# A fused attention and MLP block: three transposes taken from TensorE to VectorE and DMA

## The chip, the cores and the metric

The kernel runs on one core of one Trainium2 chip. The metric is the device time of one execution in microseconds (us). The time before is the median of three runs; the profile is of one further execution.

## The reference

x is one sequence of S = 2048 tokens with D = 576 features, in f32. With `x = layernorm(A_x)` as the common input, the result is a sum of a sliding attention branch and of a mixing and MLP branch:

```python
def _A_ref(x, wqkv, wo):          # 32 heads of 18, window 8, dilation 2
    q, k, v = split(x @ wqkv)     # 576 x 1728
    # each token attends to itself and 7 tokens before it, 2 apart
    attn = softmax(einsum(q, k_gathered) * 18 ** -0.5 + mask)
    return einsum(attn, v_gathered) @ wo

def _B_ref(x, w1, w2, w3, w4):
    h = gelu(layernorm(x) @ w1)               # 576 x 576
    # four quarters of the features, shifted by +1, -1, +2, -2 tokens
    x1 = x + shifted(h) @ w2                  # 576 x 576
    return x1 + gelu(layernorm(x1) @ w3) @ w4 # 576 x 4608, 4608 x 576

xn = layernorm(A_x)
return A_x + _A_ref(xn, wqkv, wo) + _B_ref(xn, w1, w2, w3, w4)
```

## The kernel before, in words

Tokens come in 16 tiles of 128 and in 4 blocks of 512. Every f32 matmul is done as three matmuls of fp32r parts: an operand is split into `hi` (cast on ScalarE) and `lo` (the rest, subtracted on VectorE), and the products hi x hi, hi x lo and lo x hi are added in PSUM. 576 features are four chunks of 128 and a tail of 64; a transposed block `xt` has nine slots: 0 to 3 the `hi` of the chunks, 5 to 8 their `lo`, and slot 4 the tail, `hi` in the upper 64 partitions and `lo` in the lower 64. `PAIRS` (line 35) lists the 14 products, so a group is 14 matmuls, or 28 where two PSUM banks are filled.

Four arrays have to be transposed so that features lie on the partitions: x (normalised), z (normalised again, the input of w1), x1n (x1 normalised, the input of w3) and o (the attention's result, the input of wo). In the kernel before all four go through `transposes` (line 97): four TensorE transposes of 128 x 128 per token tile (line 102), and for every second tile one more for the tails of a pair (line 105), into PSUM; from there a cast on ScalarE (107, 110) and a subtract on VectorE (111, 114) write the nine slots.

The order is written out by hand, one program order for all engines:

- **Q stage** (lines 298 to 347). x is loaded, normalised (`norm_x`), transposed (`prep_x`) and multiplied by wqkv; the result is spilled to DRAM (`spill`, line 217). The first z tiles are normalised and transposed within the last four token tiles (336 to 347). Transposed blocks lie in a ring of two buffers (`ring_block`, 167).
- **Mixing** (422 to 440). Per block, four groups of 14 matmuls (`mix_tile`) and one of 9 for the remainder (`mix_rem`), with two gelus and a subtract each. `mix_rem` returns five small VectorE and ScalarE steps, which `todo` hands out one by one and which fill T4. The z tiles of the next block are transposed in between (429). Mixing uses the two one-bank PSUM buffers `psa`.
- **w2 loop** (481 to 505). Per token tile 28 matmuls, an add onto `Y`, the statistics (`stats`, line 84), and for tiles 6 to 13 the normalising and transposing of x1n (`n_norm`, `n_prep`). The rest of `todo` is handed out here.
- **MLP** (697 to 742). 72 units (18 pairs of hidden chunks x 4 blocks) of two `up` groups (line 612) and the unit before's four `down` groups (625). x1n's tiles 8 to 15 are normalised and transposed in units 0 to 2 (`LATE`, 645). Beside it VectorE computes the attention: a generator (516) hands out its instructions, each with a cost in us; `bg` (597) is called six times per unit with the credit `RATE / 6` and stops when the credit is spent. The generator is opened in unit 1, gets credit from unit 3, and is flushed at unit NU - 4 = 68. Its result goes to DRAM as `od` (554).
- **End** (743 to 768). o's tiles are loaded from `od` (`load_o`), transposed (`prep_o`), x is added to `Y` (695), and per tile 28 matmuls with wo, an add and a store follow.

All DMAs are issued by SyncE's queue (SP), in program order; an issue that waits holds those behind it.

Of the kernel before, what the change touches and what calls it, by code (L numbers as in the profile page):

```python
# [8 lines left out]
F32 = mybir.dt.float32  # L9
# [36 lines left out]
def fused_block(ctx, tc, x, wqkv, wo, w1, w2, w3, w4, out):  # L46
# [19 lines left out]
    BN = base.tile([128, 4, 2, 6], F32, name="bn")  # L66
    qkvd = dram.tile([24, HALO + S, GC], F32, name="qkvd")
# [4 lines left out]
    def tail_half(t):  # L72
        if t % 2 == 0:
            ztail[t // 2] = base.tile([128, 128], F32, name="ztail", bufs=2)
        return ztail[t // 2][:, t % 2 * 64:t % 2 * 64 + 64]

    def norm_z(dst, kind, t):
        norm(dst, Y[:, t, :512], kind, t)
        norm(tail_half(t), Y[:, t, 512:], kind, t)
# [4 lines left out]
    def stats(src, kind, t):  # L84
        st = BN[:, bncnt[0] % 4]
        bncnt[0] += 1
        for h in range(2):
            dve.bn_stats(out=st[:, h, :], in_=src[:, h * HF:(h + 1) * HF])  # L88
        dve.bn_aggr(out=MV[kind][:, t, :], in_=st)
        dve.tensor_scalar(RS[kind][:, t, 0:1], MV[kind][:, t, 1:2], 1e-5, None, op0=ALU.add)  # L90
        pool.tensor_tensor(RS[kind][:, t, 1:2], RS[kind][:, t, 0:1], mhalf, op=ALU.pow)

# [23 lines left out]

    def split_w(dst_hi, dst_lo, raw):
        act.copy(dst_hi, raw)  # L118
        dve.tensor_tensor(dst_lo, raw, dst_hi.bitcast(F32), op=ALU.subtract)
# [20 lines left out]
    zp = {}  # L140

    def z_norm(t):
        zp[t] = w1pool.tile([128, 512], F32, name="z", bufs=2)
        norm_z(zp[t], 1, t)

    def z_prep(t):
        xt = ring_block(("z", t // 4))
        transposes(zp[t], pair_tail(ztail[t // 2], xt, t), xt, (t % 4) * 128)
# [87 lines left out]
    def q_half(t, h):  # L236
        ps = psb.tile([128, 2, 512], F32, name="ps", tag="b")
        mm_tok(ps, lhs(t), lambda b, i: WQ[:, b, (2 * h + i) * CG:(2 * h + i + 1) * CG], CG)
        stg = qpool.tile([128, 2 * CG], F32, name="stg", bufs=4)
        act.copy(stg.rearrange("p (i c) -> p i c", i=2), ps[:, :, :CG])  # L240
        spill(stg, t, 2 * h * CG, 2 * CG)
# [84 lines left out]
    for t in range(4, NT):  # L326
        for h in range(2):
            q_half(t, h)
            if h == 0:
                if t + 2 < NT:  # L330
                    x_stage(t + 2)
                    if t + 4 < NT:
                        load_x(t + 4)
                    if t + 3 < NT:
                        stats(xtile[t + 3], 0, t + 3)
                if t >= NT - 2:
                    z_prep(2 * (t - NT + 2) + 1)
                    z_norm(2 * (t - NT + 2) + 3)
                if t in (5, 6):
                    split_w1(t - 5)  # L340
            else:
                if t == NT - 4:
                    z_norm(0)
                    z_norm(1)
                if NT - 3 <= t < NT - 1:
                    z_prep(2 * (t - NT + 3))
                    z_norm(2 * (t - NT + 3) + 2)
# [13 lines left out]
    pool.memset(T4[:, S:S + 4].bitcast(F32), 0.0)  # L361

    def load_w2(k):
        r = mpool.tile([128, D], F32, name="rz", tag="rz", bufs=2)
        if k < 4:
            sp.dma_start(r, w2[k * 144:k * 144 + 128, :])
        else:
            for g in range(4):
                for a in range(2):
                    sp.dma_start(r[32 * g + 16 * a:32 * g + 16 * a + 16, :],  # L370
                                 w2[144 * g + 128:144 * g + 144, :])
        return r
# [3 lines left out]
    def mix_tile(b, m):  # L376
        xt = xring[("z", b)]
        ps = psa.tile([128, 512], F32, name="p1", tag="a")
        for i, (a, w) in enumerate(PAIRS):
            pe.matmul(ps, W1[:, w, m * 128:(m + 1) * 128], xt[:, a, :],  # L380
                      start=i == 0, stop=i == len(PAIRS) - 1)
        g32 = mpool.tile([128, 512], F32, name="g32", bufs=1)
# [8 lines left out]
    def mix_rem(b):  # L391
        xt = xring[("z", b)]
        ps = psa.tile([128, 512], F32, name="p1", tag="a")
        for a in range(9):
            pe.matmul(ps, W1R[:, a if a < 5 else a - 5, :], xt[:, a, :], start=a == 0, stop=a == 8)  # L395
        u = mpool.tile([128, 512], F32, name="u", bufs=2)
        v = mpool.tile([128, 512], F32, name="v", bufs=2)
        act.copy(u, ps)
# [21 lines left out]
    w2raw[0] = load_w2(0)  # L420
    w2raw[1] = load_w2(1)
    for b in range(NB):
        for i, m in enumerate((0, 1, 2, 4, 3)):
            nz = 4 * (b + 1) + i
# [4 lines left out]
            if b + 1 < NB and i < 4:  # L429
                z_prep(nz)  # L430
                if nz + 2 < NT:
                    z_norm(nz + 2)
            if todo and (i in (1, 2) or len(todo) > 5):
                todo.pop(0)()
            k = {(0, 1): 0, (0, 2): 1, (0, 4): 2, (1, 4): 3, (2, 4): 4}.get((b, i))
            if k is not None:
                split_w(W2[:, k, :], W2[:, 5 + k, :], w2raw[k])
                if k < 3:
                    w2raw[k + 2] = load_w2(k + 2)
    w1p.__exit__(None, None, None)  # L440
# [28 lines left out]
    def n_norm(t, zpool):  # L469
        zp[t] = zpool.tile([128, D], F32, name="rz", tag="rz", bufs=2)[:, :512]  # L470
        norm_z(zp[t], 2, t)

    def n_prep(t):
        xt = x1n.get(t // 4)
        if xt is None:
            xt = x1n[t // 4] = ring_block(("n", t // 4))
        transposes(zp[t], pair_tail(ztail[t // 2], xt, t), xt, (t % 4) * 128)

    load_f(0)
    load_f(1)  # L480
    for t in range(NT):
        ps = psb.tile([128, 2, 512], F32, name="ps", tag="b")
        if 6 <= t < 14:
            n_norm(t - 6, mpool)
# [17 lines left out]
        if 6 <= t < 14:  # L502
            n_prep(t - 6)
        if 2 <= t and todo:
            todo.pop(0)()
# [6 lines left out]
    hp = ctx.enter_context(tc.tile_pool(name="hp", bufs=2, reuse_waits="tile"))  # L512

# [98 lines left out]
    def up(c, b, i):  # L612
# [7 lines left out]
        act.activation(hi, ps, AF.Gelu_apprx_tanh)  # L620
        act.activation(g32, ps, AF.Gelu_apprx_tanh)  # L621
# [25 lines left out]
    oT = {}  # L647
# [25 lines left out]
    otile, xagain = {}, {}  # L673

    def load_o(t):
        if t % 2 == 0 and t < NT:
            src = od[t * 128:(t + 2) * 128, :].rearrange("(a p) d -> p a d", a=2)
            otile[t // 2] = opool.tile([128, 2, 512], F32, name="ot", bufs=2)
            sp.dma_start(otile[t // 2], src[:, :, :512])
            ztail[t // 2] = base.tile([128, 128], F32, name="ztail", bufs=2)  # L680
            sp.dma_start(ztail[t // 2].rearrange("p (a c) -> p a c", a=2), src[:, :, 512:])

    def load_xa(t):
        if t < NT:
            xagain[t] = opool.tile([128, D], F32, name="xa", bufs=2)
            sp.dma_start(xagain[t], xf[t * 128:(t + 1) * 128, :])

    def prep_o(t):
        if t >= NT:
            return  # L690
        oT[t] = opool.tile([128, 9, 128], F32R, name="oT", bufs=3)
        o = otile[t // 2]
        tail = (ztail[t // 2], [(oT[t - 1], 0), (oT[t], 0)]) if t % 2 else None
        transposes(o[:, t % 2, :], tail, oT[t], 0)
        dve.tensor_tensor(Y[:, t, :], Y[:, t, :], xagain[t], op=ALU.add)

    for u, (c, b) in enumerate(units):
        if u == 1:
# [3 lines left out]
        r = RATE[b] / 6 if u >= 3 else 0.0  # L702
        if u == NU - 4:
            while not state["done"]:
                bg(1e9)
            open_wo()
            load_wo(0)
            load_wo(2)
        if u == NU - 3:
            split_wo(0)  # L710
            load_wo(4)
            load_o(0)
            load_o(2)
            load_xa(0)
            load_xa(1)
# [4 lines left out]
        for i in range(C):  # L720
            bg(r, False)
            ts = LATE.get((u, i), ())
            for t in ts:
                n_norm(t, hp)
            up(c, b, i)
            for t in ts:
                n_prep(t)
# [22 lines left out]
    for t in range(NT):  # L750
        yv = Y[:, t, :].rearrange("p (h c) -> p h c", h=2)
        if t < NT - 1:
            ps = psb.tile([128, 2, 512], F32, name="ps", tag="b")
            mm_tok(ps, lambda a, t=t: oT[t][:, a, :], lambda b, h: Wo[:, b, h * HF:(h + 1) * HF], HF)
            prep_o(t + 3)
            load_xa(t + 5)
            load_o(t + 6)
            dve.tensor_tensor(yv, ps[:, :, :HF], yv, op=ALU.add)
            sp.dma_start(of[t * 128:(t + 1) * 128, :], Y[:, t, :])
        else:  # L760
            for h in range(2):
                ph = psa.tile([128, 512], F32, name="p1", tag="a")
                for i, (a, b) in enumerate(PAIRS):
                    pe.matmul(ph[:, :HF], oT[t][:, a, :], Wo[:, b, h * HF:(h + 1) * HF],  # L764
# [31 lines left out]
```

## Time and profile before

| | |
|---|---|
| median of 3 runs | 1322.93 us (1322.83 to 1323.02) |
| the profiled execution's own time | 1322.94 us |
| its span | 1321.2 us |
| granted TensorE clock | 1.00 |
| TensorE busy | 1312.1 us |
| VectorE busy | 921.9 us |
| ScalarE busy | 348.2 us |
| DMA traffic | 93.76 MB, 71 GB/s on average |

Rows of a group read: line, engine, operation, output <- input by the program's names, shapes, count, then busy us, mean ns of one, then the idle time of the engine ahead of them and what ended it. PE is TensorE's matmul, PEld its weight load, DVE VectorE, ACT ScalarE, POOL GpSimd, SP SyncE, SPq the issue of a DMA on SP. Matmuls overlap, so a row's mean is longer than what one adds to the time; the chain that ended last shows the latter. The span is what the profile covers; the small rest up to the time lies around it.

### The profile page before, as it was taken

Reading aid. Unit: us, or ns where it says so; the run is one execution under the profiler, and the core shown is the slowest. Engines: PE = TensorE matmul, PEld = TensorE weight load, DVE = VectorE, ACT = ScalarE, POOL = GpSimd, SP = SyncE. Lnnn points to the kernel's source line nnn. Section 1 sums busy time; section 2 is a strip of 40 time slices with the busy share of each in tenths; the row PEclk is TensorE's granted clock in tenths of the full one; section 3 lists DMA queues with packets and bytes.
Section 4 is the critical chain, followed back from the end, with each engine's and each line's share of the span. In section 5 each row is a group of like instructions: output and inputs, shape, how many; then the busy total and the mean of one; then the engine's idle time right before and its main releaser. Section 6 shows DMA issues by size and latency. Waiting matters only on the chain.

```text
span 1321.2 us, 18855 instructions
## 1 busy us (share of the span) xinstructions
PE 1312.1 (99%) x7894; PEld 1208.0 (91%) x7894; DVE 921.9 (70%) x1332; ACT 348.2 (26%) x633; POOL 35.2 (3%) x92
## 2 busy tenths in 40 slices
PE   8999999999999999999999999999999999999998
PEld 8999998899899999999999999999999999999998
DVE  6443326687676778878868868878877886884454
ACT  4322225411423222222122222223213223122111
POOL 2010100011000000000000000000000000000000
PEclk9999999999999999999999999999999999999999
DMA  7644322020112021221221220220320200212164
GB/s 211 152 107 108 98 68 69 18 82 28 59 30 80 20 71 39 71 71 39 71 71 29 80 71 20 90 71 20 90 71 19 82 28 20 71 42 95 46 192 140
DMA packets 120325, 93.76 MB, mean 71 GB/s; under 512 B 73504, under 2 KB 100000, under 8 KB 120240
## 3 DMA queue, kind: packets, MB, share of 16 engines
q1 hardware_dynamic: 120240, 92.56, 23.9%
q8 instruction: 62, 1.02, 0.3%
q14 instruction: 23, 0.19, 0.0%
HBM read 67.83 MB, written 23.66 MB: 69 GB/s over the span
## 4 chain that ended last, share of the span: by engine, by line
PE 96%; DVE 2%; ACT 1%; SPq 1%; issue 1%; DMA 0%; POOL 0%; DVEq 0%; ACTq 0%; POOLq 0%
PE ps L636 34%; PE p L616 34%; PE ps L133 18%; PE ps L230 3%; PE p L380 3%; PE ps L102 2%; PE p L272 0%; PE p L395 0%; PE p L764 0%; DVE bn L88 0%; PE ps L105 0%; ACT xt L107 0%; DVE xt L111 0%; SPq L370 0%; DVE xt L114 0%
## 5 line engine op out<-in xcount | busy, mean ns | idle before, releaser
L636 PE MATMUL ps<-W,hi 128*128 128x288 f32 x2304 | 397.9, 294 | 0.5 <-DVE oT L114 0.5
L636 PEld LDWEIGHTS ps<-W,hi 128*128 128x128 f32 x2304 | 339.5, 188 | 6.1 <-PE ps L102 0.7
L620 ACT ACTIVATE hi<-p 128x512 fp32r<-128x512 f32 x144 | 86.2, 599 | 619.3 <-PE p L616 619.3
L636 PE MATMUL ps<-W,lo 128*128 128x288 f32 x1152 | 245.3, 294 | 0.0
L616 PE MATMUL p<-xt,W 128*128 128x512 f32 x1008 | 235.4, 390 | 0.0
L616 PE MATMUL p<-x1n,W 128*128 128x512 f32 x1008 | 234.9, 389 | 0.0
L622 DVE TENSOR_TENSOR lo<-g,hi 128x512 fp32r<-128x512 f32 x144 | 99.7, 692 | 193.2 <-ACT g L621 193.2
L639 DVE TENSOR_TENSOR Y<-ps,Y 128x576 f32<-128x576 f32 x288 | 212.8, 751 | 16.3 <-PE ps L636 16.1
L616 PEld LDWEIGHTS p<-x1n,W 128*128 128x128 f32 x1008 | 187.2, 188 | 36.8
L616 PEld LDWEIGHTS p<-xt,W 128*128 128x128 f32 x1008 | 187.1, 188 | 36.9
L636 PEld LDWEIGHTS ps<-W,lo 128*128 128x128 f32 x1152 | 185.4, 187 | 0.0
L133 PE MATMUL ps<-WQ,xt 128*128 128x432 f32 x672 | 135.3, 360 | 0.0
L133 PEld LDWEIGHTS ps<-WQ,xt 128*128 128x128 f32 x672 | 125.2, 188 | 5.2
L111 DVE TENSOR_TENSOR xt<-ps,xt 128x512 fp32r<-128x512 f32 x40 | 27.6, 689 | 87.2 <-ACT xt L110 52.1
L568 DVE TENSOR_TENSOR prod<-q,k 128x1152 f32<-128x1152 f32 x64 | 86.5, 1351 | 0.0
L571 DVE TENSOR_REDUCE L<-prod 128x64 f32<-128x1152 f32 x64 | 86.2, 1347 | 0.0
L621 ACT ACTIVATE g<-p 128x512 f32<-128x512 f32 x144 | 85.4, 593 | 0.0
L548 DVE TENSOR_TENSOR prod<-v,L 128x1152 f32<-128x1152 f32 x56 | 75.6, 1350 | 0.0
L552 DVE TENSOR_TENSOR o<-o,prod 128x1152 f32<-128x1152 f32 x56 | 75.6, 1350 | 0.0
L118 ACT CAST W<-rawf 128x640 fp32r<-128x640 f32 x72 | 50.5, 702 | 68.9 <-PE ps L636 62.2
L133 PE MATMUL ps<-Wo,oT 128*128 128x288 f32 x420 | 59.1, 298 | 0.2
L133 PEld LDWEIGHTS ps<-Wo,oT 128*128 128x128 f32 x420 | 56.2, 188 | 1.4 <-issue 1.4
(103 smaller groups left out, 941.9 us busy)
## 6 DMA issues: line engine op xcount, KB each, us to landing
qkvd<-stg SPq DMA_DIRECT2D x24, 432.0 KB, 3.4
rawf<-in_B_w_dram SPq DMA_DIRECT2D x36, 288.0 KB, 3.0
rawf<-in_B_w_dram SPq DMA_DIRECT2D x36, 256.0 KB, 2.9
xin<-in_A_x_dram SPq DMA_DIRECT2D x16, 288.0 KB, 3.8
q<-qkvd SPq DMA_DIRECT2D x8, 576.0 KB, 3.8
k<-qkvd SPq DMA_DIRECT2D x8, 576.0 KB, 5.7
v<-qkvd SPq DMA_DIRECT2D x8, 576.0 KB, 5.9
od<-o SPq DMA_DIRECT2D x8, 576.0 KB, 4.9
```

Of the source, the lines that this page charges most:

```text
L118: act.copy(dst_hi, raw)
L133: pe.matmul(ps[:, h, :n], xs(a), ws(b, h), start=i == 0, stop=i == len(PAIRS) - 1)
L548: dve.tensor_tensor(dst, vv, Lf[:, :, w:w + 1].to_broadcast([128, TPP * GH, HD]), op=ALU.mult)
L552: dve.tensor_tensor(o, o, dst, op=ALU.add)
L568: dve.tensor_tensor(prod.rearrange("p (j h) d -> p j (h d)", h=GH), q, k[:, r0:r0 + TPP, :], op=ALU.mult)
L571: dve.tensor_reduce(Lf[:, :, w], prod, axis=AX.X, op=ALU.add)
L616: pe.matmul(ps, W3[f][:, w, :], x1n[b][:, a, :], start=n == 0, stop=n == len(PAIRS) - 1)
L620: act.activation(hi, ps, AF.Gelu_apprx_tanh)
L621: act.activation(g32, ps, AF.Gelu_apprx_tanh)
L622: dve.tensor_tensor(lo, g32, hi.bitcast(F32), op=ALU.subtract)
L636: pe.matmul(ps[:, k, :HF], h[:, col], w[:, p, k * HF:(k + 1) * HF], start=n == 0, stop=n == len(seq) - 1)
L639: dve.tensor_tensor(yv, ps[:, :, :HF], yv, op=ALU.add)
```

## The change

x is transposed as before. z, x1n and o are not transposed on TensorE any more.

- `turn` (two VectorE instructions) transposes a token tile in squares of 32 x 32 into a staging tile `ST` of a whole block; the tail is written twice. `put` spills `ST` to DRAM in four DMAs of 32 partitions, in runs of 128 floats, so that DRAM holds the block transposed; `get` fetches it into slots 4 to 8 of a block in two DMAs. `split_x` then makes `hi` and `lo` in place: four ScalarE copies and three VectorE subtracts per block, or in two parts. `room` makes one `ST` and one `RT` for each of the stages.
- Within a block the tokens come out in another order (quarter, tile, 32 tokens). `in_order` and `by_token` put it right when a gelu or a copy reads PSUM; o's tokens are loaded in such an order (`quads`) that the transposed block has them in sequence.
- z: tiles are normalised and turned two per token tile at tiles 6 to 13 of the Q stage; block 0 is fetched at tile 12 and split at 14, block 1 is fetched at the end of the Q stage, blocks 2 and 3 in mixing.
- x1n is normalised on ScalarE (`n_turn`), for which `stats` computes the bias with one more VectorE and one more GpSimd instruction. Tiles 0 to 11 are turned in the w2 loop, 12 to 15 in MLP unit 0.
- Mixing uses the PSUM buffers `psb`, and all of `todo` is handed out within it; w2's raw tiles have a pool of their own and are loaded within mixing.
- The attention is opened in unit 2, gets credit from unit 4 at 6.1 in place of 5.9 a unit, and is flushed at unit NU - 5 = 67. x is added to `Y` within the MLP, one tile each four units. o is loaded by blocks into two buffers from unit 67 on and turned in units 68 to 71.

```diff
+    def turn(src, t):
+        c = slice(32 * t, 32 * t + 32)
+        dve.transpose(ST[:, 4:20, c], src[:, :512].rearrange("p (j c) -> p j c", c=32))
+        dve.transpose(ST[:, 0:4, c].rearrange("p (a j) c -> p a j c", a=2),
+                      src[:, 512:].rearrange("p (j c) -> p j c", c=32)[:, None, :, :]
+                      .to_broadcast([128, 2, 2, 32]))
+    def put(key):
+        xd[key] = dram.tile([5, 128, 512], F32, name="xd", bufs=4)
+        for q in range(4):
+            sp.dma_start(dram_ap(xd[key], 128 * q, [[512, 32], [32 * 512, 20], [1, 128]]),
+                         ST[32 * q:32 * q + 32])
+    def get(key, xt):
+        for k in ((0, 3), (3, 5)):
+            sp.dma_start(xt[:, 4 + k[0]:4 + k[1], :].bitcast(F32),
+                         xd[key][k[0]:k[1]].rearrange("k p c -> p k c"))
+    def split_x(xt, part=None):
+        raw = xt.bitcast(F32)
+        if part != 1:
+            act.copy(RT[64:128, :], raw[64:128, 4, :])
+            act.copy(xt[0:64, 4, :], raw[0:64, 4, :])
+            dve.tensor_tensor(xt[64:128, 4, :], raw[64:128, 4, :], RT[64:128, :].bitcast(F32),
+                              op=ALU.subtract)
+        for h in range(2) if part is None else (part,):
+            hi, lo = slice(2 * h, 2 * h + 2), slice(2 * h + 5, 2 * h + 7)
+            act.copy(xt[:, hi, :], raw[:, lo, :])
+            dve.tensor_tensor(xt[:, lo, :], raw[:, lo, :], raw[:, hi, :], op=ALU.subtract)
+    def in_order(blk):
+        return blk.rearrange("p (q t c) -> p t q c", q=4, t=4)
+    def by_token(blk):
+        return blk.rearrange("p (t q c) -> p t q c", q=4, t=4)
...
+                if t == 12:
+                    get(("z", 0), ring_block(("z", 0)))
+                if t == 14:
+                    split_x(xring["z", 0])
+            elif 6 <= t < 14:
+                z_turn(2 * t - 12)
+                z_turn(2 * t - 11)
+                if t % 2:
+                    put(("z", (t - 7) // 2))
...
-        act.activation(hi, ps, AF.Gelu_apprx_tanh)
-        act.activation(g32, ps, AF.Gelu_apprx_tanh)
+        act.activation(by_token(hi), in_order(ps), AF.Gelu_apprx_tanh)
+        act.activation(by_token(g32), in_order(ps), AF.Gelu_apprx_tanh)
...
-        for i, m in enumerate((0, 1, 2, 4, 3)):
+        for i, m in enumerate((0, 1, 2, 4, 3) if b < 3 else (4, 0, 1, 2, 3)):
...
-            if b + 1 < NB and i < 4:
-                z_prep(nz)
...
+            if b + 1 < NB and i in (1, 2):
+                split_x(xring["z", b + 1], i - 1)
+            for _ in range((0, 1, 1, (1, 2, 2, 2, 3)[i])[b]):
                 todo.pop(0)()
+            if b + 2 < NB and i == 4:
+                get(("z", b + 2), ring_block(("z", b + 2)))
...
+    def n_turn(t, zpool):
+        z = zpool.tile([128, D], F32, name="rz", tag="rz")
+        act.activation(z, Y[:, t, :], AF.Identity, bias=RS[2][:, t, 0:1], scale=RS[2][:, t, 1:2])
+        turn(z, t % 4)
+        if t % 4 == 3:
+            put(("n", t // 4))
...
-        if 6 <= t < 14:
-            n_prep(t - 6)
-        if 2 <= t and todo:
-            todo.pop(0)()
+        if 2 <= t < 6:
+            n_turn(t - 2, rzpool)
+        if t in (9, 10, 13, 14):
+            k = {9: 4, 10: 6, 13: 8, 14: 10}[t]
+            n_turn(k, rzpool)
+            n_turn(k + 1, rzpool)
+        if t in (8, 13):
+            x1n[t // 13] = ring_block(("n", t // 13))
+            get(("n", t // 13), x1n[t // 13])
+        if t in (11, 15):
+            split_x(x1n[t // 15])
...
-    RATE = [5.9, 5.9, 5.9, 5.9]
+    RATE = [6.1, 6.1, 6.1, 6.1]
-    LATE = {(0, 0): (8, 9), (0, 1): (10, 11), (1, 0): (12,), (1, 1): (13,), (2, 0): (14,), (2, 1): (15,)}
+    LATE = {(0, 0): (12, 13), (0, 1): (14, 15)}
...
+            if (u, i) in ((0, 0), (1, 0)):
+                get(("n", u + 2), x1n[u + 2])
+            for t in LATE.get((u, i), ()):
+                n_turn(t, tp)
+            if u in (1, 2):
+                split_x(x1n[u + 1], i)
...
                 down(*prev, j)
+                if u >= NU - 4:
+                    o_turn(u - NU + 4, j)
+                if u >= NU - 2 and j == 1:
+                    split_x(xo[u - NU + 2])
+            if u >= NU - 4:
+                load_o(u - NU + 6)
+            if u >= NU - 3:
+                get(("o", u - NU + 3), o_block(u - NU + 3))
...
+        if 4 <= u < 4 + 4 * NT:
+            if u % 4 == 0:
+                load_xa(u // 4 - 1)
+            if u % 4 == 2:
+                add_x(u // 4 - 1)
...
     for j in range(4):
-        if j < 3:
-            prep_o(j)
-            load_xa(j + 2)
         down(*prev, j)
-    load_o(4)
+    split_x(xo[2])
...
+        if t == 1:
+            get(("o", 3), o_block(3))
+        if t == 5:
+            split_x(xo[3])
```

More of the change, by code (lines that the diff above doesn't have):

```diff
@@ L73, in tail_half @@
         if t % 2 == 0:
-            ztail[t // 2] = base.tile([128, 128], F32, name="ztail", bufs=2)
+            ztail[t // 2] = qpool.tile([128, 128], F32, name="ztail", bufs=2)
         return ztail[t // 2][:, t % 2 * 64:t % 2 * 64 + 64]
-    def norm_z(dst, kind, t):
-        norm(dst, Y[:, t, :512], kind, t)
-        norm(tail_half(t), Y[:, t, 512:], kind, t)
     def pair_tail(src, xts, t):
@@ L91, in stats @@
         pool.tensor_tensor(RS[kind][:, t, 1:2], RS[kind][:, t, 0:1], mhalf, op=ALU.pow)
+        if kind == 2:
+            neg = MV[kind][:, t, 0:1]
+            dve.tensor_scalar(neg, neg, -1.0, None, op0=ALU.mult)
+            pool.tensor_tensor(RS[kind][:, t, 0:1], neg, RS[kind][:, t, 1:2], op=ALU.mult)
     def norm(dst, src, kind, t):
@@ L115, in transposes, with room, quads @@
                               xtt[0:64, 4, ct:ct + 128].bitcast(F32), op=ALU.subtract)
+    def room(p):
+        nonlocal ST, RT
+        ST = p.tile([128, 20, 128], F32, name="st")
+        RT = p.tile([128, 512], F32R, name="rt")
+    def turn(src, t):
[28 more added lines that the diff above has]
+        return blk.rearrange("p (t q c) -> p t q c", q=4, t=4)
+    def quads(t_, b, q):
+        return dram_ap(t_, (512 * b + 128 * q) * D, [[D, 32], [32 * D, 4], [1, D]])
     def split_w(dst_hi, dst_lo, raw):
@@ L139, in fused_block, with z_turn @@
     W1R = w1pool.tile([128, 5, 128], F32R, name="W1R")
[L140 to L148, printed above, removed]
+    room(w1pool)
+    def z_turn(t):
+        z = w1pool.tile([128, D], F32, name="z", bufs=1)
+        norm(z, Y[:, t, :], 1, t)
+        turn(z, t % 4)
     qp = tc.tile_pool(name="qp", bufs=1, reuse_waits="tile")
@@ L240, in q_half @@
         act.copy(stg.rearrange("p (i c) -> p i c", i=2), ps[:, :, :CG])
+        if t == NT - 1 and h == 1:
+            get(("z", 1), ring_block(("z", 1)))
         spill(stg, t, 2 * h * CG, 2 * CG)
@@ L439, in fused_block @@
                     w2raw[k + 2] = load_w2(k + 2)
+    assert not todo
+    mup.__exit__(None, None, None)
     w1p.__exit__(None, None, None)
@@ L467, in fused_block @@
     x1n = {}
[L469 to L477, printed above, removed]
+    def n_turn(t, zpool):
+        z = zpool.tile([128, D], F32, name="rz", tag="rz")
+        act.activation(z, Y[:, t, :], AF.Identity, bias=RS[2][:, t, 0:1], scale=RS[2][:, t, 1:2])
+        turn(z, t % 4)
+        if t % 4 == 3:
+            put(("n", t // 4))
     load_f(0)
     load_f(1)
+    nsp = tc.tile_pool(name="nsp", bufs=1, reuse_waits="tile")
+    room(nsp.__enter__())
     for t in range(NT):
         ps = psb.tile([128, 2, 512], F32, name="ps", tag="b")
-        if 6 <= t < 14:
-            n_norm(t - 6, mpool)
         def xs(a, t=t):
@@ L512, in fused_block @@
     hp = ctx.enter_context(tc.tile_pool(name="hp", bufs=2, reuse_waits="tile"))
+    tp = ctx.enter_context(tc.tile_pool(name="tp", bufs=1, reuse_waits="tile"))
+    room(tp)
     apc = tc.tile_pool(name="ap", bufs=1, reuse_waits="tile")
@@ L671, in split_wo, with load_o, o_turn, o_block @@
                 worw[k][:, :n * D].rearrange("p (k c) -> p k c", k=n))
[L673 to L681, printed above, removed]
-    def load_xa(t):
[L684 to L694, printed above, removed]
+    otile, xagain, xo = {}, {}, {}
+    def load_o(b):
+        if b < NB:
+            otile[b] = opool.tile([128, 4, D], F32, name="ot", bufs=2)
+            for q in range(4):
+                sp.dma_start(otile[b][32 * q:32 * q + 32], quads(od, b, q))
+    def load_xa(t):
+        xagain[t] = tp.tile([128, D], F32, name="rz", tag="rz")
+        sp.dma_start(xagain[t], xf[t * 128:(t + 1) * 128, :])
+    def o_turn(b, t):
+        turn(otile[b][:, t, :], t)
+        if t == 3:
+            put(("o", b))
+    def o_block(b):
+        if b < 2:
+            xo[b] = ring_block(("o", b))
+        else:
+            xo[b] = xp.tile([128, 9, 512], F32R, name=f"x1n{b}")
+        return xo[b]
+    def add_x(t):
         dve.tensor_tensor(Y[:, t, :], Y[:, t, :], xagain[t], op=ALU.add)
     for u, (c, b) in enumerate(units):
-        if u == 1:
+        if u == 2:
             ap_pool = apc.__enter__()
@@ L762, in fused_block @@
                 ph = psa.tile([128, 512], F32, name="p1", tag="a")
-                for i, (a, b) in enumerate(PAIRS):
-                    pe.matmul(ph[:, :HF], oT[t][:, a, :], Wo[:, b, h * HF:(h + 1) * HF],
+                for i, (a, w) in enumerate(PAIRS):
+                    pe.matmul(ph[:, :HF], oT(a), Wo[:, w, h * HF:(h + 1) * HF],
                               start=i == 0, stop=i == len(PAIRS) - 1)
```

72 lines of the change are left out of this document (29 added, 43 removed).

## The prediction

> **What bounds the kernel now.** I read the page's busy times first, then its chain of work that ended last, then a table of windows by stage, then the chain in order of time.
>
> ```profile
> span 1321.2 us, 18855 instructions
> PE 1312.1 (99%) x7894; PEld 1208.0 (91%) x7894; DVE 921.9 (70%) x1332; ACT 348.2 (26%) x633; POOL 35.2 (3%) x92
> PE 96%; DVE 2%; ACT 1%; SPq 1%; issue 1%; DMA 0%; POOL 0%; DVEq 0%; ACTq 0%; POOLq 0%
> PE ps L636 34%; PE p L616 34%; PE ps L133 18%; PE ps L230 3%; PE p L380 3%; PE ps L102 2%; PE p L272 0%; PE p L395 0%; PE p L764 0%; DVE bn L88 0%; PE ps L105 0%; ACT xt L107 0%; DVE xt L111 0%; SPq L370 0%; DVE xt L114 0%
> ```
>
> TensorE is busy 99% of the span and makes 96% of the chain; no other engine is near. So the time falls only by TensorE instructions that go, or by TensorE's few stalls. Lines 102 and 105 on the chain are TensorE's own transposes. The change takes most of them away and adds no matmul.
>
> The stages, from the table of windows (columns: window and its length, then busy us and count of PE, PEld, DVE, ACT, POOL, then the granted clock, DMA share, GB/s). They are the mixing (w1), the w2 loop with the MLP's first four `up` groups, the rest of the MLP, and the end: four last `down` groups and the o projection.
>
> ```profile
> 196.96:264.08 67.12, 66.30 (x317) 54.12 (x316) 43.09 (x80) 35.40 (x71) 0.76 (x18) 1.00 0.16 43
> 264.08:345.22 81.14, 80.21 (x569) 76.35 (x569) 64.44 (x149) 18.55 (x41) 12.52 (x24) 1.00 0.22 68
> 345.22:1241.84 896.62, 896.62 (x5379) 819.34 (x5379) 687.29 (x802) 225.24 (x384) 0.00 (x0) 1.00 0.17 54
> 1241.84:1317.95 76.11, 75.38 (x568) 73.69 (x566) 41.79 (x69) 12.73 (x32) 0.00 (x0) 1.00 0.51 162
> ```
>
> TensorE idles 0.82, 0.93, 0.00 and 0.73 us here, at a granted clock of 1.00. It isn't waiting; it is full.
>
> What a piece of work costs on TensorE, from the chain in order of time (start, length, what):
>
> ```profile
> 196.96 3.20 PE p L380 x14
> 200.16 0.44 PE ps L102 x4
> 204.26 0.11 PE ps L105
> 208.04 2.09 PE p L395 x9
> 365.36 6.35 PE p L616 x28
> 384.50 6.34 PE ps L636 x48
> 1254.65 3.72 PE ps L133 x28
> ```
>
> A 512-wide group of 14 matmuls takes 3.20 (mixing) or 3.18 (half of 6.35, MLP), the remainder group 2.09, four `down` groups 6.34, a w2 or o token tile 3.72. A token tile's four transposes take 0.44, a pair's tail 0.11: 0.11 a transpose. One MLP unit is 6.35 + 6.34 = 12.7 us.
>
> **What goes.** The groups by shape count the transposes.
>
> ```profile
> L102 PE MATMUL ps<-ident,rz 128*128 128x128 f32 x64 | 9.6, 276 | 0.9 <-DVE rz L94 0.7
> L102 PE MATMUL ps<-ident,z 128*128 128x128 f32 x64 | 9.6, 272 | 0.0
> L102 PE MATMUL ps<-ident,ot 128*128 128x128 f32 x64 | 9.6, 272 | 0.0
> L105 PE MATMUL ps<-ident,ztail 128*128 128x128 f32 x30 | 8.2, 272 | 0.0
> ```
>
> 192 transposes of z, x1n (`rz`) and o, and 24 of the 30 tails (x keeps 6): 216. They overlap, so I take the chain's 0.11 and not the row's 0.27: 216 x 0.11 = 23.8 us. That is the lower end. The upper end compares each stage with what its matmuls alone take:
>
> - Q stage, four z tiles: 4 x 0.44 + 2 x 0.11 = 2.0.
> - Mixing: 16 x 3.20 + 4 x 2.09 = 59.6 of 67.12 leaves 7.5.
> - w2 loop and four `up`: 16 x 3.72 + 4 x 3.18 = 72.2 of 81.14 leaves 8.9.
> - Rest of the MLP, two x1n tiles: 1.0.
> - End: 6.34 + 16 x 3.72 = 65.9 of 76.11 leaves 10.2.
>
> Together 29.6. The 5.8 beyond the transposes are idle time (2.5) and slower restarts of the matmuls behind a transpose. I take the upper end, since the long MLP window, almost without transposes, has no idle time.
>
> **What comes in their place.** A tile of z, x1n or o is turned by two VectorE instructions (512 wide, and the 64-wide tail written twice, 128), four DMAs per block of 512 tokens spill it, two DMAs fetch it transposed, then one split per block replaces four casts and subtracts from PSUM. No row shows a VectorE transpose. Rows that bound it:
>
> ```profile
> L94 DVE TENSOR_SCALAR z<-Y,mv,rs 128x512 f32<-128x512 f32 x16 | 8.7, 542 | 0.2
> L165 DVE COPY ztail<-Y 128x64 f32<-128x64 f32 x12 | 2.4, 196 | 0.4
> L111 DVE TENSOR_TENSOR xt<-ps,xt 128x512 fp32r<-128x512 f32 x40 | 27.6, 689 | 87.2 <-ACT xt L110 52.1 <-ACT xt L107 34.6 <-issue 0.3
> L114 DVE TENSOR_TENSOR xt<-ps,xt 64x128 fp32r<-64x128 f32 x40 | 11.6, 289 | 0.8
> L538 DVE RECIPROCAL mx<-mx 128x64 f32<-128x64 f32 x8 | 4.4, 554 | 0.3
> L119 DVE TENSOR_TENSOR Wo<-rawf,Wo 128x1152 fp32r<-128x1152 f32 x2 | 2.7, 1350 | 0.0
> L118 ACT CAST Wo<-rawf 128x1152 fp32r<-128x1152 f32 x2 | 2.3, 1153 | 0.0
> L639 DVE TENSOR_TENSOR Y<-ps,Y 128x576 f32<-128x576 f32 x288 | 212.8, 751 | 16.3 <-PE ps L636 16.1
> L621 ACT ACTIVATE g<-p 128x512 f32<-128x512 f32 x144 | 85.4, 593 | 0.0
> ```
>
> Low end: one-source rows, 0.54 + 0.20 = 0.75 us a tile. High end: the reciprocal, 0.554 / 64 = 8.7 ns an element, 640 elements, 5.5 us. I take 0.75, nearest in kind: one source, same width. A block split is, on VectorE, 0.69 (64 x 512) + 2 x 1.35 x 1024 / 1152 = 3.1 us; on ScalarE 2 x 0.59 + 2 x 1.02 = 3.2. VectorE loses 0.69 + 0.29 a tile in subtracts, 3.9 a block, and for x1n also the normalisation, which ScalarE takes over: about 0.67 by 576 / 512 of 0.593. So VectorE's sum hardly changes: per block 4 x 0.75 + 3.1 against 3.9 before, 2.2 more, less the 3 us or so of normalisation of each x1n block. ScalarE, 26% busy, has room.
>
> The gelus now read PSUM in runs of 32. No row shows that. Nothing lost, or at worst twice 0.593: four of them in a 12.7 us unit would then be 4.8, still hidden.
>
> Mid-MLP, VectorE gets attention at 6.1 instead of 5.9 a unit, and an add of x (0.75) every fourth unit:
>
> ```profile
> 995.00:1046.00 51.00, 51.00 (x307) 46.60 (x307) 42.41 (x48) 14.57 (x24) 0.00 (x0) 1.00 0.20 58
> L554 SPq DMA_DIRECT2D od<-o x8: 562/562/612, 530.8 to 1184.7; - x8
> ```
>
> 42.41 of 51 us, the fullest kind of window, is 10.6 of a 12.7 us unit; plus 0.2 and 0.2 makes 11.0: hidden. Attention now starts one unit later and must end one earlier. I counted the generator's written costs against the credit: it ends in unit 67 of 71 now (the last `od` write, 1184.7, is in unit 67, which runs from 1178 to 1191), and in unit 65 after; the flush stands at unit 67. So nothing is flushed.
>
> **The new waits.** Each block passes turn, spill, fetch, split before its first matmul. DMA rows (KB each, us to landing):
>
> ```profile
> qkvd<-stg SPq DMA_DIRECT2D x24, 432.0 KB, 3.4
> v<-qkvd SPq DMA_DIRECT2D x8, 576.0 KB, 5.9
> raw<-in_B_w_dram SPq DMA_DIRECT2D x1, 864.0 KB, 5.8
> ```
>
> And VectorE's other work around them:
>
> ```profile
> L88 DVE BATCH_NORM_STATS2 bn<-Y 128x6 f32<-128x288 f32 x64 | 26.2, 451 | 0.7
> L89 DVE BATCH_NORM_AGGREGATE mv<-bn 128x2 f32<-128x12 f32 x48 | 10.0, 209 | 1.6
> L414 DVE SCALAR_TENSOR_TENSOR T<-v,sgn,u 32x512 fp32r<-32x512 f32 x16 | 11.9, 746 | 0.6
> L119 DVE TENSOR_TENSOR W<-rawf,W 128x640 fp32r<-128x640 f32 x36 | 29.6, 822 | 0.0
> L119 DVE TENSOR_TENSOR W<-rawf,W 128x576 fp32r<-128x576 f32 x36 | 27.0, 749 | 0.0
> ```
>
> A spill is 4 x 320 KB: 3.4 and three issues of about 0.5, say 5. A fetch is 768 + 512 KB: 6 to 9. SP issues in order: a fetch that waits holds later weight loads and spills, but those are issued units ahead.
>
> - z blocks: block 0 is spilled early in the Q stage. Blocks 1 to 3 are fetched into the ring when the matmuls of the tile they replace end, land 6 to 9 later, and are needed one mixing block (14.9 us) later, with some 4 us of split: 2 to 5 us to spare.
> - x1n blocks 0 and 1 are spilled within the w2 loop; block 1's split stands behind the last tile's add and statistics (0.75 + 2 x 0.45 + small ones), so its last subtract ends about 5.5 us after the last w2 matmul, and unit 1 starts after 6.35.
> - x1n block 2 is tightest. Tile 11 is turned when the last w2 matmul ends (T0). Spill lands T0 + 5, fetch T0 + 11 to 14, the split's second half, behind a gelu pair on ScalarE, ends T0 + 17 to 20. Unit 2 starts T0 + 6.35 + 12.7 = T0 + 19.
> - x1n block 3 is spilled in unit 0 and needed at T0 + 32; o blocks have a whole unit each.
> - The last T4 pieces move from the w2 loop into mixing; their VectorE work (3 x 0.75) ends about 4 us after mixing, and tile 0 reads T4 after 3.2. It costs 1 us if the wait covers the whole tile, nothing if only the columns.
>
> I put 2 us on these (from 0 to about 8).
>
> **The sum.** 1321.2 - 29.6 + 2 = 1293.6 us of span. The profiled execution took 1322.94 and stands 0.01 from the median 1322.93; 1.7 lie outside the span. Forecast: 1295 us.
>
> **Rivals.**
>
> - *Gaps stay.* Only the transposes go (23.8) and restarts cost as before: 1322.9 - 23.8 + 1 = 1300. For it: the 5.8 were not traced to single waits.
> - *Late hand-offs.* If landings run at twice those rows, block 2 is about 8 late, z blocks and T4 2 to 3: 1295 + 10 = 1305. For it: spill and fetch share the DMA engines with weight loads; the DMA share in the last stage is 0.51. Against: 0.16 to 0.22 in the stages where margins are thin.
> - *The transposing DMA is slow*, the same mechanism far on: when a spill takes some 30 us more, x1n block 2 alone is late by the whole gain. Against: the `qkvd` spill writes runs of 72 floats (288 bytes) and lands in 3.4; this one writes runs of 128 floats. [...]
> - *Slower: VectorE becomes the bound* at its transposes. In the w2 loop it has 59.5 us, of which adds (16 x 0.75), statistics (16 x 1.4: two of 0.45, 0.21 and small ones), the weight splits of two f (2 x 1.57) and two block splits (6.2) take 44; 12 turns share 15.5, 1.3 each. In each of the last four units adds, `lo` subtracts (2 x 0.69), a weight split (1.35) and a block split leave 3.9 of 12.7 for four turns, 0.97 each. Beyond, a turn of d us costs 12 (d - 1.3) + 16 (d - 0.97). The gain is gone at d = 2.1; at d = 3, four passes of 0.75, the cost is 53: 1348.
> - *The transposes weren't on the end's path*: no change, 1323. The chain speaks against it.
>
> **How the numbers follow.** Forecast, 1291 to 1298: 0.62. Gaps stay: 0.14. Late hand-offs, to 1312: 0.14. No change: 0.03. Slower, by VectorE 0.06, by a slow DMA 0.01. A measurement of this kernel tells 0.2% (2.6 us) from no change; so faster 0.90, same 0.03, slower 0.07. The range runs from 1291 (all of the 29.6 and no new wait is 1293.3; 2 below that for the cadences, which are read off single pieces) to 1307, which takes in the gaps and most of the late hand-offs.
>
> **What would show it.** Right: rows of line 102 only for Y; mixing about 60 us, w2 loop to first `down` about 73, end about 67; TensorE near 99%; VectorE's transposes near 0.55 and 0.2. Wrong: TensorE waiting for `xt` or `x1n` subtracts or casts at a block's first matmul, above all unit 2's; `ps` rows waiting for VectorE in the last four units; transposes above 1 us; a flush of attention at unit 67.

## The result, and the profile after

The changed kernel takes 1322.41 us (median of 20 runs, 1320.25 to 1324.73) against 1323.01 before: a ratio of 0.9997, interval 0.9990 to 1.0004. No change that can be measured; the forecast was 1295. The transposes are gone, and so is what they cost, but it was given back at the end. The page's top and chain:

```profile
span 1320.6 us, 18507 instructions
PE 1291.7 (98%) x7678; PEld 1191.0 (90%) x7678; DVE 936.0 (71%) x1336; ACT 362.0 (27%) x601; POOL 38.3 (3%) x108
PE   8999999999999999999999999999999999999599
PEclk9999999999999999999999999999999999999699
PE 91%; DMA 3%; DVE 3%; SPq 1%; ACT 1%; issue 1%; DVEq 0%; ACTq 0%
```

TensorE is busy 20.4 us less than before (1312.1), in a span that is 0.6 shorter. One slice of the forty, the 38th, is half empty, and the clock granted falls in the same place. The windows by stage (columns as in the prediction; the unit numbers follow from the chain):

```profile
194.87:253.86 58.99, 58.99 (x262) 48.82 (x262) 35.09 (x48) 36.02 (x59) 0.76 (x18) 1.00 0.41 118
253.86:325.84 71.98, 71.98 (x504) 69.76 (x504) 59.82 (x148) 27.48 (x38) 14.24 (x40) 1.00 0.55 138
325.84:334.52 8.68, 6.78 (x50) 6.54 (x49) 6.41 (x8) 4.72 (x7) 0.00 (x0) 1.00 0.88 214
334.52:1173.96 839.44, 839.44 (x5018) 766.05 (x5017) 672.01 (x778) 212.72 (x358) 0.00 (x0) 1.00 0.22 68
1173.96:1218.26 44.30, 44.30 (x258) 39.90 (x257) 22.98 (x40) 9.30 (x15) 0.00 (x0) 1.00 0.60 137
1218.26:1267.42 49.16, 29.35 (x181) 28.33 (x179) 23.51 (x36) 11.89 (x17) 0.00 (x0) 0.79 0.50 130
1267.42:1317.36 49.94, 49.93 (x364) 49.69 (x364) 13.79 (x18) 3.14 (x4) 0.00 (x0) 0.97 0.34 119
```

Mixing takes 58.99 instead of 67.12, the w2 loop with four `up` groups 71.98 instead of 81.14, both without idle time. In the first `down` groups (third row) TensorE stands 1.9 us. The MLP is full again up to unit 68, which starts at 1173.96 instead of 1191.04: 17.1 us ahead. From there to the last matmul the kernel before needed this (one window of its trace):

```profile
1191.04:1317.95 126.91, 126.18 (x872) 120.09 (x871) 62.97 (x97) 24.75 (x52) 0.00 (x0) 1.00 0.37 118
```

The changed one needs 44.30 + 49.16 + 49.94 = 143.4, 16.5 more, with 69 matmul records fewer (803 against 872). Of 49.16 us in the sixth row TensorE works 29.35: 19.8 us idle, at a mean granted clock of 0.79.

Some pieces of the chain of the end, in order of time (start, length, what), show what it stands for:

```profile
1206.65 1.80 SPq L137
1208.49 1.89 SPq L738
1214.08 7.34 DMA xt<-xd
1221.44 0.61 ACT rt L148
1224.82 1.22 DVE xt L155
1226.04 0.68 DVE Y L699
1226.76 6.49 PE ps L696 x35
1233.25 8.49 DMA xt<-xd
1246.42 0.68 DVE Y L699
1247.14 6.50 PE ps L696 x35
1253.64 8.37 DMA x1n<-xd
```

Read each round from its end backwards: a `down` group (L696) waits for a PSUM buffer, which the add onto Y (L699) frees; that add stands in VectorE's queue behind a split (L155), the split behind ScalarE's copies (L148 to L154), the copies behind the block's fetch. And the fetch starts late because of SP's queue (its DMA issues in order of time, one line of `Wo` loads left out):

```profile
1189.38 4.81 SPq L137 DMA_DIRECT2D xd<-st  x4
1194.23 4.41 SPq L738 DMA_DIRECT2D ot<-od  x4
1204.31 4.14 SPq L137 DMA_DIRECT2D xd<-st  x4
1208.49 5.49 SPq L738 DMA_DIRECT2D ot<-od  x4
1214.08 0.91 SPq L142 DMA_DIRECT2D xt<-xd  x2
1228.99 4.16 SPq L137 DMA_DIRECT2D xd<-st  x4
1233.25 3.57 SPq L142 DMA_DIRECT2D xt<-xd  x2
```

o block 0 is spilled at 1189.4, but fetched only at 1214.1 (L142), behind the next spill (L137) and the load of another block (L738), each of which holds SP for 4 to 5 us. Block 1 likewise: spilled at 1204.3, fetched at 1233.3, behind block 2's spill. To the issuing comes waiting: the spills of blocks 1 to 3 wait 30.8 us in all (at most 13.9) for their block's last turn on VectorE, and the fetch of the block before stands behind them. So the delay feeds itself: the turns of block 2 stand on VectorE behind the split that waits for block 0's fetch.

### The profile page after: what moved, and what is told of

Read it like the earlier page. It is cut to its first block, busy times and chain, and to the rows that moved or that the text cites. A ratio compares the mean times of both kernels' runs of the same rounds, so it can differ in the third digit from the quotient of the medians.

```text
span 1320.6 us, 18507 instructions
## 1 busy us (share of the span) xinstructions
PE 1291.7 (98%) x7678; PEld 1191.0 (90%) x7678; DVE 936.0 (71%) x1336; ACT 362.0 (27%) x601; POOL 38.3 (3%) x108
## 4 chain that ended last, share of the span: by engine, by line
PE 91%; DMA 3%; DVE 3%; SPq 1%; ACT 1%; issue 1%; DVEq 0%; ACTq 0%
PE ps L696 33%; PE p L676 32%; PE ps L182 17%; PE ps L431 4%; PE ps L276 3%; DMA xt<-xd 1%; DMA x1n<-xd 1%; DMA xd<-st 1%; SPq L137 1%; PE ps L446 1%; DVE st L129 1%; PE ps L104 1%; DVE Y L699 0%; SPq L738 0%; DVE bn L86 0%
## 5 line engine op out<-in xcount | busy, mean ns | idle before, releaser
L696 PE MATMUL ps<-W,hi 128*128 128x288 f32 x2304 | 402.4, 296 | 19.2 <-DVE Y L699 19.2
L696 PEld LDWEIGHTS ps<-W,hi 128*128 128x128 f32 x2304 | 342.8, 189 | 26.5 <-DVE Y L699 13.9
L696 PE MATMUL ps<-W,lo 128*128 128x288 f32 x1152 | 246.8, 296 | 0.0
L699 DVE TENSOR_TENSOR Y<-ps,Y 128x576 f32<-128x576 f32 x288 | 212.5, 750 | 16.0 <-PE ps L696 16.0
L696 PEld LDWEIGHTS ps<-W,lo 128*128 128x128 f32 x1152 | 186.8, 189 | 0.0
L168 DVE TENSOR_TENSOR W<-rawf,W 128x640 fp32r<-128x640 f32 x72 | 56.3, 785 | 0.0
L182 PE MATMUL ps<-W,h 128*128 128x288 f32 x384 | 53.5, 295 | 0.0
L182 PEld LDWEIGHTS ps<-W,h 128*128 128x128 f32 x384 | 51.9, 188 | 0.1
```

Of the source, the lines that this page charges most:

```text
L182: pe.matmul(ps[:, h, :n], xs(a), ws(b, h), start=i == 0, stop=i == len(PAIRS) - 1)
L696: pe.matmul(ps[:, k, :HF], h[:, col], w[:, p, k * HF:(k + 1) * HF], start=n == 0, stop=n == len(seq) - 1)
```

## The experiments

**Theory A**: the loss is made by waits in program order in units 68 to 71: SP holds each fetch behind the next spill; ScalarE and VectorE stand at a split or at a turn with gelus and PSUM adds queued behind. **Theory B**: the DMA engines are full there (share 0.92 to 0.97 in the 26 us from 1193), and the order doesn't matter. **Theory C**: the lower clock after a stop is itself the loss. All times are medians beside runs of the kernel before on the same chip (1322.8 to 1322.9).

**e1_fetch_first**

```diff
+        if u >= NU - 3:
+            get(("o", u - NU + 3), o_block(u - NU + 3))
         if prev is not None:
...
-            if u >= NU - 3:
-                get(("o", u - NU + 3), o_block(u - NU + 3))
```

> o block b's fetch is issued ahead of block b+1's spill and of the next load of o, once the unit's up groups are issued; nothing else moves. Theory A (waits in order: SP holds each fetch behind the next spill, and ScalarE and VectorE stand at the split of that block with gelus and PSUM adds behind them): the splits of o blocks 0 and 1 no longer wait; what stays are VectorE's waits for the staging tile to be spilled. In the trace of the changed kernel the first o projection group starts at 1253.6; I work out about 1240 here, so about 1309 us (1306 to 1313). Theory B (the DMA engines are full at the end: share 0.92 to 0.97 at 215 GB/s, so the same bytes take the same time in any order): 1319 to 1323, unchanged. Theory C (the clock granted after an idle stretch is the loss itself): the loss falls only as far as idle stretches go, so as A, but with less than the idle time gained.

Measured: 1308.74 us, ratio 0.9890 (0.9875 to 0.9905). As A said, and against B: the same bytes in another order take 13.7 us less.

**e2_late_split**

```diff
-                if u >= NU - 2 and j == 1:
-                    split_x(xo[u - NU + 2])
...
     for j in range(4):
         down(*prev, j)
-    split_x(xo[2])
+        if j == 1:
+            split_x(xo[0])
+    split_x(xo[1])
...
-        if t == 5:
-            split_x(xo[3])
+        if t in (3, 7):
+            split_x(xo[2 + t // 7])
```

> DMA order as in the changed kernel, but the splits of o blocks come later in program order: block 0 within the last four down groups, block 1 behind them, blocks 2 and 3 at o tiles 3 and 7. Theory A: the fetches land as late as before, but no gelu and no PSUM add stands behind a split that waits; spills of blocks 2 and 3 come earlier since VectorE is free; first o group at about 1236 instead of 1253.6, so about 1305 us (1302 to 1311). Theory B: the fetches of blocks 2 and 3 come too late and TensorE waits at o tiles 8 or 12; 1315 to 1323.

Measured: 1304.01 us, 0.9859 (0.9842 to 0.9875). Here no DMA is issued in another order; only what stands behind a wait is changed. That is worth 18.4 us.

**e3_both**: the two edits together.

> Both edits: fetches issued ahead of the next spill, and the splits late. Theory A: as the better of the two, and what remains are VectorE's waits for the one staging tile (3.5, 5.1 and 6.3 us in the changed kernel), which hold adds of the last units: 1300 to 1307 us. Theory B: 1315 to 1323.

Measured: 1303.16 us, 0.9850 (0.9835 to 0.9864), hardly less than e2 alone: both take away the same wait. What is left, from the waits between 1170 and 1275 (who for whom: total us, times, longest):

```profile
DVE st L129 <- DMA xd<-st: 12.4, 2, 6.2
DVE st L129 <- issue: 4.9, 1, 4.9
PE ps L696 <- DVE Y L699: 5.9, 1, 5.9
```

No split waits for a fetch any more in this stretch. The turns (L129) still wait for the staging tile to be spilled, and TensorE for the adds behind them.

**e4_o_tensor**: o back to TensorE's transposes, from tile loads as before the change, into the freed ring and x1n buffers; the rest as changed.

```diff
-                if u >= NU - 4:
-                    o_turn(u - NU + 4, j)
...
     for j in range(4):
+        if j < 3:
+            prep_o(j)
         down(*prev, j)
...
+            prep_o(t + 3)
+            load_o(t + 6)
```

> z and x1n by VectorE and DMA as in the changed kernel, o alone back to TensorE transposes and tile loads (x still added within the MLP). Theory A and B alike, as both place the whole loss in o's path: the gain that the changed kernel has at unit 68 (17.1 us, 1173.96 against 1191.04) stays: 1322.9 - 17 = 1306 us (1304 to 1308). If instead something in the earlier stages cost time later, or the end of the kernel is slow for another reason (the clock, the loads of wo), it stays near 1315 to 1322.

Measured: 1305.51 us, 0.9868 (0.9853 to 0.9882). The gain of z and x1n is real and stays; o's part alone cost 16.9 us as it was written.

**e5_turn_last**, on e3_both: `for j in range(4): o_turn(...)` behind the loop of the four `down`.

> On top of e3_both: in the last four units the four turns of an o block stand behind the unit's four adds instead of between them. Theory A: what is left of the loss in e3_both is one stop of 5.9 us and a slow restart, where adds stand behind a turn that waits for the staging tile's spill. Here the adds go first; the last block's turns still hold the adds of the final down groups, so TensorE stops for about 4 us instead: 1301 us (1299 to 1303). If turns that wait are not the cause, 1303 as e3_both.

Measured: 1300.59 us, 0.9832 (0.9819 to 0.9846), as expected; the one stop left in the end is 3.0 us.

**e6_early**, on e3_both: loads, turns and fetches of o one unit earlier.

```diff
-        if u == NU - 5:
+        if u == NU - 6:
...
-                if u >= NU - 4:
-                    o_turn(u - NU + 4, j)
+                if NU - 5 <= u < NU - 1:
+                    o_turn(u - NU + 5, j)
```

> On top of e3_both: o is loaded from unit 66 and turned in units 67 to 70, one unit earlier (the attention's flush moves to unit 66; by its written costs it ends in unit 65). Theory A: every spill has landed before VectorE needs the staging tile again or it holds only early units' adds; the 5.9 us stop and its slow restart (about 2 us) go: 1295 us (1293 to 1298). Theory B (DMA engines full at the end): as e3_both, 1303.

Measured: 1300.24 us, 0.9826 (0.9812 to 0.9839): 3 less than e3_both, not the 8 expected. VectorE's and TensorE's timelines show how the slack was used up (some rows; idle time ahead in brackets):

```profile
1185.39 0.71 DVE L129 STREAM_TRANSPOSE st<-ot 128x512 f32<-128x512 f32 x1 [2.03 <-DMA ot<-od]
1205.38 0.71 DVE L129 STREAM_TRANSPOSE st<-ot 128x512 f32<-128x512 f32 x1 [7.64 <-DMA xd<-st]
1220.23 0.71 DVE L129 STREAM_TRANSPOSE st<-ot 128x512 f32<-128x512 f32 x1 [6.49 <-DMA xd<-st]
```

```profile
1206.98 0.80 PE L696 MATMUL ps<-W,hi 128*128 128x288 f32 x4 [0.73 <-DVE Y L699]
1213.80 0.80 PE L696 MATMUL ps<-W,hi 128*128 128x288 f32 x4 [1.79 <-DVE Y L699]
1228.06 0.79 PE L696 MATMUL ps<-W,hi 128*128 128x288 f32 x4 [1.20 <-DVE Y L699]
```

The first turns of the four blocks stand at 1171.3, 1185.4, 1205.4 and 1220.2, so 14 to 20 us apart against 12.7 of a unit. The second waited for its load of o, the last two for the staging tile: with one such tile a block's turns, its spill's issues and their landing follow each other. An earlier start doesn't shorten that period. Theory A needed this amendment; e8_two_stage tests it.

**e7_all**, on e6_early: x1n block 2 split between unit 1's `down` groups, and `add_x` one unit later.

> On top of e6_early: x1n block 2 is split between the down groups of unit 1 instead of ahead of them, so that the adds don't all stand behind its late fetch (1.9 us of TensorE in the changed kernel), and the add of x comes at the end of every fourth unit's next one, away from a w3 split (13 stops of 0.1 us). Theory A: 2 to 4 us less than e6_early: 1292 us (1290.5 to 1294.5), near the sum of the prediction without new waits, 1293.3.

Measured: 1301.17 us, 0.9836 (0.9822 to 0.9849): no gain. The stop among unit 1's `down` groups was gone and came back one unit later, at block 3, whose split still stood ahead of the adds: TensorE's one wait near there is

```profile
345.57 0.80 PE L696 MATMUL ps<-W,hi 128*128 128x288 f32 x4 [1.94 <-DVE Y L699]
```

The clock hides part of it too: in the profiled execution the granted clock falls to a half for some 3.4 us behind this stop and again behind one of 1.80 us at 1215, some 1.7 us lost each time; e6_early's execution, at a mean clock of 1.000 against 0.997, has no such stretch. But the one run of e7_all at a clock of 1.000 takes 1299.85, within e6_early's 1298.29 to 1300.72, so no gain is shown either way. The small stops in mid-MLP, one of some 0.1 us in about every fourth unit, were not fewer either, so the cause given for them falls; they cost about 1 us in all and their cause stays open.

**e8_two_stage**, on e3_both: two staging tiles in turn, the second in a ring buffer that x1n block 0 has left.

```diff
+        if t == 0:
+            ST = sts[b % 2]
...
+            xs = ring.tile([128, 9 * 512], F32, name="xs", tag="xt")
+            sts += [ST, xs[:, :2560].rearrange("p (j c) -> p j c", c=128)]
...
-            xo[b] = xp.tile([128, 9, 512], F32R, name=f"x1n{b}")
+            xo[b] = xp.tile([128, 9, 512], F32R, name=f"x1n{b + 1}")
```

> On top of e3_both: two staging tiles take turns in the last four units (the second lies in a ring buffer that x1n block 0 no longer needs; o's blocks use the other freed buffers). In e6_early a block still took about 15 us from one turn to the next, since the one staging tile is held by its own turns, four issues of its spill and their landing, against 12.7 us of a unit; so starting earlier only moved the stops. Theory A with this amendment: with two tiles no turn waits, the stop of 5.9 us and its slow restart (2 us) in e3_both go: 1295 us (1293.5 to 1297.5). If the stop has another cause (the loads of o, the DMA engines), 1299 to 1303.

Measured: 1296.02 us, 0.9798 (0.9784 to 0.9812), as the amended theory says. TensorE's only stop of over 0.2 us behind the mixing is the one of 1.6 us among unit 1's `down` groups.

**e9_n_late**, on e8_two_stage: both late x1n blocks split behind adds.

```diff
-            if u in (1, 2):
-                split_x(x1n[u + 1], i)
...
                 down(*prev, j)
+                if u in (1, 2) and j in (1, 2):
+                    split_x(x1n[u + 1], j - 1)
```

> On top of e8_two_stage: x1n blocks 2 and 3 are split behind the second and third down group of units 1 and 2 and not ahead of all four; e7_all did so for block 2 alone, and a stop of the same length (1.9 us) turned up one unit later, at block 3. Theory A: that stop goes: 1293.5 us (1292 to 1295). If the stop stems from the late fetch itself, which the order doesn't change, it moves to the first up group of units 2 and 3: no gain.

Measured: 1293.51 us (1293.27 to 1293.99), 0.9777 (0.9764 to 0.9791). It beats both kernels, by 29.4 us the one before. Its page, and a window from unit 68 to beyond the end (the last matmul ends at 1288.5; up to there TensorE works 116.41 of 116.45 us):

```profile
span 1291.7 us, 18507 instructions
PE 98%; DVE 1%; DMA 0%; issue 0%; ACT 0%; POOL 0%; DVEq 0%
```

```profile
1172.05:1298.00 125.95, 116.41 (x801) 111.78 (x799) 61.44 (x94) 24.59 (x36) 0.00 (x0) 1.00 0.50 147
```

The end's work takes 116.4 us of TensorE when nothing waits; the changed kernel spent 143.4 on it. So 27.0 were lost there: 19.8 idle and 7.2 in matmuls that ran slowly. The spills hold SP longer here than the 4 to 5 us in the changed kernel:

```profile
1199.40 9.01 SPq L137 DMA_DIRECT2D xd<-xs  x4
1213.09 8.49 SPq L137 DMA_DIRECT2D xd<-st  x4
```

Two spills hold it for 9.0 and 8.5 us, ScalarE waits 13.9 us for one fetch, and TensorE stands nowhere in this window. That settles B: the issues are slower here than in the changed kernel, and it costs nothing once no gelu or PSUM add stands behind them.

**e10_two_stage_alone**: two staging tiles on the changed kernel, nothing else.

> Two staging tiles alone, on the changed kernel: fetches still behind the next spill, splits of o blocks 0 and 1 still early. Theory A: only VectorE's waits for the staging tile go (3.5, 5.1 and 6.3 us); the splits still wait for late fetches with gelus and adds behind them; by working the queue through, the first o group starts at about 1247 instead of 1253.6: 1316 us (1313 to 1319). If the staging tile is the main cause, below 1305; if it is none, 1322.

Measured: 1317.57 us, 0.9965 (0.9952 to 0.9978). The second tile alone is worth 4.8 us, on top of e3_both 7.1; the late splits alone 18.4. The waiting splits are the larger part, the staging tile the smaller.

## Why the prediction was wrong

- **What goes: right, in size too.** 29.6 us for transposes, idle time and restarts gave 1293.3 without new waits; e9_n_late, in which TensorE doesn't wait for the new hand-offs, takes 1293.5. By stage it gains 1.9 (Q stage), 8.1 (mixing), 9.0 (w2 loop), 0.0 (MLP up to unit 68) and 10.5 us (end); forecast were 2.0, 7.5, 8.9, 1.0 and 10.2. The upper end was the one to take, and *gaps stay* fell; that the totals agree within 0.2 us is partly luck, since the misses of the stages cancel.
- **What comes on VectorE and ScalarE: sizes off, no matter.** Groups by shape of the changed kernel:

```profile
L129 DVE STREAM_TRANSPOSE st<-ot 128x512 f32<-128x512 f32 x16 | 11.2, 699 | 14.9 <-DMA xd<-st 6.3 <-DMA ot<-od 5.1 <-issue 3.5
L130 DVE STREAM_TRANSPOSE st<-ot 128x128 f32<-128x128 f32 x16 | 4.3, 270 | 0.0
L523 ACT ACTIVATE rz<-Y,rs 128x576 f32<-128x576 f32 x16 | 13.6, 869 | 39.7 <-DVE st L130 29.2 <-POOL rs L93 10.4
L155 DVE TENSOR_TENSOR xt<-xt 128x1024 fp32r<-128x1024 f32 x16 | 19.1, 1221 | 5.4 <-ACT xt L154 5.3
```

A turn takes 0.97 instead of 0.75, the normalisation on ScalarE 0.87 instead of 0.67; a split's subtract is 1.22, as worked out. VectorE's rival, which decides at 2.1 a turn, fell. The gelus are as fast as before (599 and 592 ns).
- **Attention: right.** No flush: the loads of o are issued at 1147, ahead of unit 67.
- **z, T4: right, nothing is lost** (mixing and w2 loop without idle time). **x1n block 2** was rightly named as the tightest, and cost 1.9. But TensorE did not wait for it at unit 2's first matmul: it waited among the `down` groups of unit 1, for adds that stood behind the split (L696 for L699), so that the 2 us put on all new waits fit here by luck.
- **"o blocks have a whole unit each" is the step that failed.** It counted the time between spill and use and not the queues, and so the sum had 2 us for all new waits, from 0 to about 8, where 28.9 came: 27.0 from unit 68 on and 1.9 at x1n. (One of the prediction's own signs of being wrong is what the trace shows: `ps` rows waiting for VectorE in the last four units.) The text said that a fetch which waits holds what SP issues later, and asked of no later spill whether it holds the fetch; it did not name what is queued behind a turn or a split on VectorE and ScalarE (the PSUM adds and gelus of the running unit), nor that one staging tile serves all blocks. And the issues, taken as 0.5 us, are longer (the trace's rows of the tile: issue time in ns, least, median, most; then the page's row: KB and us to landing):

```profile
L137 SPq DMA_DIRECT2D xd<-st x48: 309/1220/1825, 106.7 to 1251.7; - x48
```

```profile
xd<-st SPq DMA_DIRECT2D x48, 320.0 KB, 5.9
```

A spill was put at 5 us; o's take 8.6 to 9.4 in the changed kernel from the first issue to the last landing. A fetch queued behind one waits for its four issues, 4.1 to 4.8 us, and before that for the turns which the spill itself waits for.
- **The rival "late hand-offs" came nearest**: blocks did come late, and o's spills land 4 us later than was put. But it had slow landings as the cause and x1n and z as the place; e2_late_split makes no landing faster and takes 18.4 us less. Its price, 10 us, had neither the queues of the end nor the slow restarts. Added to 1293.3, the 1.9 and the 27.0 give 1322.2.
- The rival "no change" has the number, 1323, by luck: it held that the transposes weren't on the path, and e9_n_late shows that they were.
- The rival of the slow transposing DMA fell: it needed spills that take some 30 us more, and here, in runs of 512 bytes, all of a spill lands within 10.5 us in the changed kernel.

## What to carry to other kernels

When work moves from a full engine to DMA round trips, follow each issue through the queue of the engine that issues it, and write down what stands behind each waiting instruction on ScalarE, on VectorE and on the issuing queue itself; a wait there cost nothing here unless a gelu or a PSUM add was behind it. Put a split that waits for a fetch behind the adds of the running group, issue a fetch ahead of the next spill, and compare the period of a staging tile (fill, issue, landing) with the period of its user. A start one unit earlier took back 2.9 us where the period was too long, a second buffer 7.1; dead operand buffers at the end of a stage are room for it.

## What the runs showed of the hardware

- Behind each of the four stops at the end TensorE is slow for some 3 to 3.5 us. From the changed kernel's timeline, first with a stop of 6.76 us ahead:

```profile
1226.76 1.33 PE L696 MATMUL ps<-W,hi 128*128 128x288 f32 x4 [6.76 <-DVE Y L699]
...
1230.84 0.69 PE L696 MATMUL ps<-W,hi 128*128 128x288 f32 x4
...
1231.63 0.70 PE L696 MATMUL ps<-W,hi 128*128 128x288 f32 x4
...
1232.43 0.69 PE L696 MATMUL ps<-W,hi 128*128 128x288 f32 x4
```

The 18 matmuls from 1226.76 to 1230.84 take 4.1 us; at full speed six take 0.80 (1231.63 to 1232.43, four of one form and two of another), so 18 would take 2.4. So some 1.7 us are lost; four restarts, behind stops of 6.8, 6.1, 4.4 and 2.5 us, make up nearly all of the 7.2. The granted clock shows it: 0.50 from 1223.5, and 1.00 again from 1230.5, some 3.5 us after TensorE has restarted. The length of the stop alone doesn't decide. Behind a stop of 1.83 us in e5_turn_last the first four take 1.24 us. Behind the stops of 1.94 and 1.80 us in e7_all they take 0.80, but the clock falls to 0.50 some 0.9 and 1.5 us later, for 3.4 us. Behind stops of 1.90 us in the changed kernel and 1.79 in e6_early nothing of the kind follows. The Trainium skill (TensorE: Matmul & The Clock Gate, Part 1) puts the drop to half clock at an idle window of some 3.4 us. These traces have it behind stops of 1.8 to 3.0 us too, so a shorter stop isn't safe. As Theory C the clock explains 7.2 of the 27.0 us, not the stops.
- The issue of a DMA is not a fixed cost: the four equal 320 KB issues of block 1's spill in the changed kernel hold SP for 0.31, 0.51, 1.40 and 1.80 us, one after the other, and the fourth of block 2's in e9_n_late for 4.98.
